# Issuing an attention stage's maxima rows and loads from SyncE in a written order

## The chip, the cores and the metric

The kernel runs on one NeuronCore of a Trainium2 chip. The metric is device time in microseconds (us), the median of several executions; less is better. One execution was also taken by the hardware profiler. The engines are TensorE (PE, with its weight loads shown apart as PEld), VectorE (DVE), ScalarE (ACT), GpSimd (POOL) and SyncE (SP), which does no arithmetic here and only issues DMAs.

## The reference, cut to what matters

Three stages follow one another, all in float32: an attention over 8 batches, 8 heads, 576 positions and 64 columns with a mask by blocks of 64; a mixture of 8 experts with a capacity of 576 tokens each; and a dense layer pair with a cosine gate.

```python
scores = np.matmul(q, k.transpose(0, 1, 3, 2)) / np.sqrt(D)
scores = np.where(mask, scores, -1e9)
scores = scores - np.max(scores, axis=-1, keepdims=True)
attn = np.exp(scores); attn = attn / (attn.sum(-1, keepdims=True) + 1e-9)
x = np.matmul(attn, v)                      # then (B*S, H*D)
x = moe(x, w_gate, w1, w2)                  # 8 experts, 576 tokens each
h = x @ w_in; out = (h * np.cos(h)) @ w_out
```

The change is in the attention alone.

## The kernel before, in words

**Pairs and groups.** The attention goes through 32 pairs of heads, `p` = 0 to 31, four pairs to a batch. A group `g` = 2p + h is one head's turn, so a pair takes an even group (h = 0) and an odd one (h = 1). In a group PE makes the scores of head g (L239, L240, tile `sT`), the product of the weights of head g - 1 with v (L288, tile `av`), and the scores of head g + 4 once more, roughly, for the row maxima only (`mx_unit`, L169, tile `mx`).

**The maxima.** `mx_unit` writes five results in each group into a rotation of three PSUM banks (`mx`, bufs=3), and DVE reduces each of them to a column of maxima (L176). So the fourth result of a group needs the bank of the first, and the fifth that of the second. In the even group, `crow(p + 1)` transposes the maxima of the next pair on PE (L203), DVE negates them into a small tile `ct` (L205), and a DMA writes them as row 64 of that pair's `QK` tile (L206), where the score product reads them as one more row to sum over. That DMA is issued by POOL.

**Split q and k.** Each pair's q and k come twice: `load_max` (L87, issued by POOL) rounds them into `QK`, and `load_raw` (L103, issued by SP) brings the unrounded values into a tile `R` (two buffers). `rests` subtracts the two, half on POOL (L144) and half on DVE (L142), into the tile `QX`.

**The order of work.** The two strings `ORDER` list the steps of an even and an odd group. PE, DVE, ACT and POOL run under `manual_schedule`: each executes its own instructions in the order in which the code traces them. In an even group POOL therefore has: `load_max(p + 3)`, the row's DMA (step `c`), and `rests(p + 1, 1)` (step `rp`, L144). In an odd group it has one addition (L615). SP isn't under that rule: a scheduler placed its DMAs, which may stand before or after their place in the code; a load can be issued as soon as its buffer is free.

**Held loads.** `hold` (L350) is a copy by DVE of one element of the newest `ct` into the tile that a load is about to fill. The load then has to wait for that copy, and with it for the maxima. From group 10 on, `vT` (L153) and the weight tiles `w` (L599) are held so, at step `L`.

**Side work.** The 64-bit words of the dense layer's weights are turned into float32 on the way: for each chunk a load (L599), a `split` at the end of an odd group on DVE (L607, L608, L609), an addition on POOL two groups later (L615) and, at step `D` of the even group after that, a last DVE instruction (L627) and a store (L628). At the first pair of each batch `store_x` also adds two reductions on DVE for the router (L328, L329) and stores the finished batch.

```python
ORDER = ("x1 D s0 a0 a1 s1 c rc m0 x2 L a2 s2 m1 m2 a3 rp s3 m3 m4 k s4 a4 v rd A0",
         "x1 s0 a0 a1 s1 c rc m0 x2 a2 s2 m1 m2 B a3 s3 m3 m4 k s4 a4 v A1")
```

`x1` and `x2` are the sums and the normalization (L297, L298, L308, L310), `s` the score products with their exponentials, `a` the products with v, `m` the maxima products, `rd` the DVE half of `rests`, `A` the split, `D` the store.

Of the kernel before, what the change touches and what calls it, by code (L numbers as in the profile page):

```python
# [12 lines left out]
def _warn_once_fixed(msg, *args, **kwargs):  # L13
# [6 lines left out]
F32 = mybir.dt.float32  # L20
F32R = mybir.dt.float32r
# [3 lines left out]
OP = mybir.AluOpType  # L25
# [3 lines left out]
B, H, S, D = 8, 8, 576, 64  # L29
# [11 lines left out]

PR = dict(EC=3, E2=2, E5=7, GC=0, SI=1, NX=3, LV=3, Q0=2, WM=14, WE=0, SW=1, W0=16, WG=0, WN=5, PA=0, CS=2, sT=2, mx=3, tr=1, e32=3, RO=0, XO=0, SO=0, GO=200, TPS=4, SEP=5, L2=3, L5=9, LAG=3, WK=3, XG=5, BIG=16, GLD=99, IW=4, W1=14, CW=1, XS=6, AH=3)
PA = [(), (2, 5), (1, 3, 5), (0, 2, 4)][PR['PA']]
ORDER = ("x1 D s0 a0 a1 s1 c rc m0 x2 L a2 s2 m1 m2 a3 rp s3 m3 m4 k s4 a4 v rd A0",
         "x1 s0 a0 a1 s1 c rc m0 x2 a2 s2 m1 m2 B a3 s3 m3 m4 k s4 a4 v A1")


# [6 lines left out]
def attention(ctx, tc, qk, vv, vt, cmask, wg, xs, lg, ident, wu, side, late):  # L54
# [5 lines left out]
    nc = tc.nc  # L60
# [139 lines left out]
    def crow(p):  # L200
        n = "mx" if p < 3 else "tr"
        pt = P.tile([128, 512], F32, name=n, bufs=PR[n])
        nc.tensor.transpose(pt[0:10, 0:128], NM[p][:, 0:10], ident)  # L203
        ct = CT[p] = W.tile([10, 128], F32, name="ct")
        nc.vector.tensor_scalar(ct, pt[0:10, 0:128], -1.0, None, op0=OP.mult)  # L205
        nc.gpsimd.dma_start(QK[p % NQ][64:65, 0].rearrange("o h (c n) -> o (h c) n", c=5), ct)  # L206

    NZ = EX[2][:, 0:325].rearrange("p (c n) -> p c n", c=5)

# [138 lines left out]
    def hold(t):  # L348

        nc.vector.tensor_copy(t, CT[max(CT)][0:t.shape[0], 0:1])  # L350
# [103 lines left out]
    for g in range(NHD + 2):  # L454
        p, h = divmod(g, 2)
        b, pr = divmod(p, 4)
        on = g < NHD
        if on and b + 1 < B and g % 8 in (5, 7):
            u = 0 if g % 8 == 5 else 4
            if b == 0:  # L460
                hold(VB[1][0:1, 0, u, 0:1])
                hold(VB[1][0:1, 4, u, 0:1])
            load_v(b + 1, u, u + 4)
        if g == 0:
            start()
            continue
        if on and h == 0 and p + 1 < NP:
            if p == 2:
                hold(VT[1][0:1, 0:1])
            if p < 6:  # L470
                load_vt(p + 1)
        if on and h == 0:
            if p > 1 and p + 3 < NP:
                load_max(p + 3)
            if p == 1:
                zero(0, nc.gpsimd)
                mask(0)
            if p > 3 and p + 2 < NP:
                load_raw(p + 2)
        work = side(g)  # L480
        if on and h == 0 and 4 < p < NP - 2:
            def early(p=p):
                hold(VT[p % 2][0:1, 0:1])
                load_vt(p + 2)
            work["L"] = [early] + work.get("L", [])
        gms = [x for x in MX.get(g, [g + 4]) if x < NHD]

        def m(u):
            for x in gms:
                mx_unit(x, u)  # L490

        def s(t):
            if on:
                sc_unit(g, t)

        def a(j):
            if 0 <= g - 1 < NHD:
                av_part(g - 1, j)

        def c():  # L500
            if h == 0 and 1 < p + 1 < NP and p != 1:
                crow(p + 1)

        def x1():
            if 0 <= g - 2 < NHD:
                sums(g - 2)

        def x2():
            if 0 <= g - 2 < NHD:
                norm(g - 2)  # L510
            if g % 8 in (2, 3) and g > 3:
                store_x(b - 1, g % 8 - 2)

        more = on and 0 < p and p + 1 < NP

        def rc():
            if more:
                copies(p + 1, h)

        def rd():  # L520
            if more:
                rests(p + 1, 0)

        def rp():
            if more:
                rests(p + 1, 1)

        def v():
            q = p + 1 if h == 1 and p + 1 < NP else None
            if q is not None:  # L530
                for j in range(5):
                    vg_unit(q, j)

        def k():
            for x in gms:
                if x % 2:
                    crow_max(x // 2)

        def V():
            for j in range(5):  # L540
                vg_unit(1, j)

        did = {"P0": lambda: rest_pair(1, 0), "P1": lambda: rest_pair(1, 1), "L3": lambda: load_max(3), "L4": lambda: load_max(4),
               "R0": lambda: row_part(1, 0, 4, 1), "R1": lambda: row_part(1, 4, 5, 1), "Y0": lambda: copies(1, 0), "Y1": lambda: copies(1, 1),
               "T0": lambda: round_pair(2, 0), "T1": lambda: round_pair(2, 1), "X0": lambda: head_max(0, NM[1]), "X1": lambda: head_max(1, NM[1]), "Z": lambda: zeros(2, nc.gpsimd), "Z1": fourth, "H6": lambda: load_raw(5), "C1": lambda: crow(1), "C": lambda: crow(2),
               "H": held, "H4": later_pair, "V": V, "x1": x1, "x2": x2, "c": c, "rc": rc, "rd": rd, "rp": rp, "v": v, "k": k}
        order = ORDER[h]
        if 0 < g < 4:
            order = (FIRST, SECOND, THIRD)[g - 1]
        if g == 6:  # L550
            order = order.replace(" c ", " c H6 ")
        if g > 59:
            order = LATE if g == 60 else LATE.replace("rd rp ", "")
            if g >= NHD:
                order = "x1 a0 a1 x2 D a2 a3 a4"
        for w in order.split():
            if w in did:
                did[w]()
            elif w[0] in "ABDL":
                for f in work.pop(w[0], ()):  # L560
                    f()
            elif w[0] == "M":
                mx_unit(int(w[1]), int(w[2]))
            elif w[0] == "G":
                vg_unit(0, int(w[1]))
            elif w[0] in "sam" and len(w) == 2:
                {"s": s, "a": a, "m": m}[w[0]](int(w[1]))
        for w in work.values():
            for f in w:
                f()  # L570
        if g > 5:
            late()
# [6 lines left out]
def to_single(ctx, tc, srcs, dst):  # L579

    nc = tc.nc
    V, G = nc.vector, nc.gpsimd
    W = ctx.enter_context(tc.tile_pool(name="cv_w", bufs=2))
    C = ctx.enter_context(tc.tile_pool(name="cv_c", bufs=1))
    top = C.tile([128, 1], I32, name="top")
    V.memset(top, -(1 << 30))
    st = {}  # L590

    first = sorted(list(range(7, 64, 2)) + [6, 60, 62])

    def load(c, h=False):
        st[c] = [W.tile([128, 512, 2], I32, name="w64", bufs=3)]
        a = st[c][0]
        if h or c < 3:
            side.hold(a[0:1, 0, 0:1])
        nc.sync.dma_start(a, srcs[c].rearrange("p (n t) -> p n t", t=2))  # L599

    def split(c):
        a = st[c][0]
        hi, lo = a[:, :, 1], a[:, :, 0]
        t = W.tile([128, 512], I32, name="w32", bufs=3)
        r = W.tile([128, 512], I32, name="wrd", bufs=2)
        st[c] += [t, r]
        V.tensor_scalar(t, hi, 0x07FFFFFF, 3, op0=OP.bitwise_and, op1=OP.logical_shift_left)  # L607
        V.scalar_tensor_tensor(t, hi, top[:, 0:1], t, op0=OP.bitwise_and, op1=OP.bitwise_or)  # L608
        V.tensor_scalar(r, lo, 28, None, op0=OP.logical_shift_right)  # L609

    def rounds(c):
        a, t, r = st[c]
        nc.scalar.activation(r, r, AF.Copy, scale=0.5)
        if c < 31:
            G.tensor_tensor(t, t, r, op=OP.add)  # L615

    def size(c):
        a = st[c][0][:, :, 1].bitcast(F32)
        g = W.tile([128, 512], F32, name="wab", bufs=1) if c < 30 else a
        nc.scalar.activation(g, a, AF.Abs)  # L620
        st[c].append(g)

    def store(c):
        a, t, r, g = st.pop(c)
        if c == 31:
            V.tensor_tensor(t, t, r, op=OP.add)
        V.scalar_tensor_tensor(t.bitcast(F32), g, MIN64, t.bitcast(F32), op0=OP.is_ge, op1=OP.mult)  # L627
        nc.sync.dma_start(dst[c], t.bitcast(F32))  # L628

    def middle(c):  # L630
        rounds(c)
        size(c)

    def side(g):
        work = {}
        for c, f in enumerate(first):
            late = 2 if f > 61 else 1 if f > 58 or f < 7 else 0
            if g == f - (2 if f > 58 or f < 10 else 3):
                if 9 < g < 58 and g % 2 == 0:
                    work.setdefault("L", []).append(lambda c=c: load(c, True))  # L640
                else:
                    load(c)
            for n, d, w in (("A", f, split), ("B", f + 2 - late, middle), ("D", f + 3 - late, store)):
                if g == d:
                    work.setdefault(n, []).append(lambda w=w, c=c: w(c))
        return work
    return side
# [682 lines left out]
```

## Time and profile before

| what | value |
|---|---|
| median of 3 runs | 1683.81 us (1680.65 to 1686.99) |
| the profiled execution | 1681.19 us |
| its span, first to last instruction | 1679.3 us |
| mean granted TensorE clock | 0.990 |
| attention's even and odd groups of the middle | about 12.2 us for the two together |

The profiled execution lies 2.6 us under the median of the runs. "Busy" is the time in which an engine had an instruction of its own in work; instructions of one engine overlap by some hundredths of a microsecond at their ends. In the timelines, a bracket shows how long the engine was idle before a group of instructions and which instruction ended that.

### The profile page before, as it was taken

What the parts mean: (1) busy time and instruction counts of PE and PEld (TensorE: products, weight loads), DVE (VectorE), ACT (ScalarE), POOL (GpSimd) and SP (SyncE); (2) the same over time, 40 slices, a digit from 0 to 9 for tenths busy, and PEclk for the clock granted to TensorE, in tenths of its full rate; (3) what the DMA queues carried; (4) which work ended last, traced back from release to release, by engine and by line L of the source; (5) the groups of instructions that cost most, each with busy time, mean ns of one, the idle gap of its engine ahead of it and who ended that gap; (6) DMA issues with size and microseconds to landing.
All of it is one profiled execution on the core that took longest, in us unless ns stands there. A gap on an engine that the chain in (4) does not pass through costs nothing.

```text
span 1679.3 us, 29421 instructions
## 1 busy us (share of the span) xinstructions
PE 1655.3 (99%) x10852; PEld 1478.8 (88%) x10852; DVE 1087.9 (65%) x2946; ACT 808.7 (48%) x1622; POOL 293.9 (18%) x259
## 2 busy tenths in 40 slices
PE   9999999998899999999999999999999999999998
PEld 7999999997698898899889889988988988998886
DVE  6888888887769777676667667677554343433342
ACT  6566666664345634443442544344254344434443
POOL 7344443432124400100100100100110000000000
PEclk9999999998799999999999999999999999999999
DMA  8999899975442333423423433433433333323332
GB/s 164 293 236 233 238 253 245 232 197 184 138 157 107 119 95 107 123 96 93 132 87 100 126 88 101 132 89 104 120 120 93 99 103 98 98 84 98 113 107 82
DMA packets 112510, 230.25 MB, mean 137 GB/s; under 512 B 12989, under 2 KB 23667, under 8 KB 110339
## 3 DMA queue, kind: packets, MB, share of 16 engines
q1 hardware_dynamic: 97344, 191.21, 39.2%
q0 software_dynamic: 15024, 37.17, 9.3%
q8 instruction: 86, 1.41, 0.4%
q14 instruction: 56, 0.46, 0.1%
HBM read 192.52 MB, written 35.65 MB: 136 GB/s over the span
## 4 chain that ended last, share of the span: by engine, by line
PE 91%; issue 6%; DVE 2%; POOL 1%; ACT 0%; POOLq 0%; DVEq 0%
PE wk L1093 21%; PE acc L1118 21%; PE acc L1066 12%; PE av L288 10%; PE wk L1041 7%; PE acc L1041 4%; PE sT L239 3%; PE mx L169 3%; PE sT L240 3%; PE tr L271 2%; PE rt L1026 1%; PE rt L926 1%; PE wk L1203 1%; PE rt L800 1%; PE av L354 0%
## 5 line engine op out<-in xcount | busy, mean ns | idle before, releaser
L1118 PE MATMUL acc<-wh,big 128*128 128x512 f32 x1136 | 375.4, 392 | 0.0
L1118 PEld LDWEIGHTS acc<-wh,big 128*128 128x128 f32 x1136 | 212.6, 188 | 42.9
L1093 PE MATMUL wk<-yh,wh 128*128 128x512 f32 x576 | 227.9, 396 | 0.0
L288 PE MATMUL av<-vb,e 128*128 128x100 f32 (+1 forms) x1920 | 224.5, 259 | 0.0
L1093 PE MATMUL wk<-yh,win 128*128 128x512 f32 x576 | 224.4, 390 | 0.0
L1093 PE MATMUL wk<-yl,wh 128*128 128x512 f32 x576 | 224.4, 390 | 0.0
L1118 PE MATMUL acc<-wout,big 128*128 128x512 f32 x568 | 222.6, 392 | 0.0
L1096 ACT ACTIVATE big<-wk 128x512 int32<-128x512 f32 x144 | 85.8, 596 | 281.3 <-PE wk L1093 270.2
L1099 DVE SCALAR_TENSOR_TENSOR big<-big,wk 128x512 f32<-128x512 int32 x144 | 98.7, 685 | 186.8 <-ACT big L1096 186.7
L288 PEld LDWEIGHTS av<-vb,e 128*128 128x128 f32 (+1 forms) x1920 | 208.5, 173 | 4.1 <-ACT vb L275 0.2
L258 ACT ACTIVATE e<-sT 128x288 f32<-128x288 f32 (+3 forms) x320 | 132.3, 424 | 97.4 <-PE sT L240 90.9
L1066 PE MATMUL acc<-big,wh 128*128 128x288 f32 x1024 | 179.0, 297 | 0.0
L176 DVE TENSOR_REDUCE nm<-mx 128x1 f32<-128x288 f32 (+1 forms) x374 | 144.1, 429 | 48.7 <-PE mx L169 45.9
L993 DVE TENSOR_TENSOR wl<-wr,wh 128x512 fp32r<-128x512 f32 x128 | 88.2, 691 | 108.2 <-PE acc L1066 38.1
L1127 POOL DMA_INDIRECT out<-big,idx x36 | 35.7, 993 | 681.4 <-ACT big L1124 673.6
L1066 PEld LDWEIGHTS acc<-big,wh 128*128 128x128 f32 x1024 | 149.9, 189 | 0.1
L1104 DVE TENSOR_TENSOR big<-wk,big 128x512 f32<-128x512 f32 x144 | 99.3, 690 | 78.0 <-ACT big L1101 77.7
L992 ACT ACTIVATE wh<-wr 128x512 fp32r<-128x512 f32 x128 | 81.0, 633 | 106.0 <-DMA wr<-in_w 38.5
L239 PE MATMUL sT<-qk 128*128 128x288 f32 (+5 forms) x384 | 128.2, 343 | 0.4 <-ACT qk L220 0.2
L1093 PEld LDWEIGHTS wk<-yh,win 128*128 128x128 f32 x576 | 108.1, 188 | 22.9
L1093 PEld LDWEIGHTS wk<-yh,wh 128*128 128x128 f32 x576 | 108.5, 188 | 21.2
L1093 PEld LDWEIGHTS wk<-yl,wh 128*128 128x128 f32 x576 | 108.3, 188 | 20.9
(255 smaller groups left out, 3105.8 us busy)
## 6 DMA issues: line engine op xcount, KB each, us to landing
wh<-hs SPq DMA_DIRECT2D x256, 256.0 KB, 2.6
wr<-in_w SPq DMA_DIRECT2D x128, 256.0 KB, 2.7
R<-in_qk SPq DMA_DIRECT2D x30, 576.0 KB, 6.8
qk<-in_qk POOLq DMA_DIRECT2D x29, 576.0 KB, 6.2
vT<-in_vt SPq DMA_DIRECT2D x32, 288.0 KB, 3.9
w<-in_win SPq DMA_DIRECT2D x16, 512.0 KB, 5.2
ws<-w SPq DMA_DIRECT2D x32, 256.0 KB, 4.1
xs<-X SPq DMA_DIRECT2D x16, 512.0 KB, 7.3
```

Of the source, the lines that this page charges most:

```text
L176: RED.append(nc.vector.tensor_reduce(m[:, c:c + 1], ps[:, o:o + n], axis=AX.X, op=OP.max))
L239: nc.tensor.matmul(out, lhsT=a[0:r, 1, h, k], rhs=a[0:r, 0, h, 64 + q0:64 + q0 + n], start=True, stop=False)
L258: nc.scalar.activation(e[:, o:o + n], ps[:, 0:n], AF.Exp, scale=0.125)
L288: nc.tensor.matmul(AV[hg % 2][0:n, c, w], lhsT=E32[hg][:, q:q + n], rhs=v[:, (j * H + hd) * 73 - o + w.start:(j * H + hd) * 73 - o + w.sto ...
L993: V.tensor_sub(l,raw,h.bitcast(F32))
L1041: nc.tensor.matmul(ps[q][:,0:288],lhsT=w[:,128*d:128*d+128],rhs=x[:,d,288*q:288*q+288],start=d==0 and n==0,stop=d==3 and n==2)
L1066: nc.tensor.matmul(ps[q][:,0:288],lhsT=w[:,sl],rhs=x[:,288*q:288*q+288],start=f==0 and n==0,stop=f==7 and n==2)
L1093: nc.tensor.matmul(ps,lhsT=w[:,sl],rhs=y[:,d,:],start=d==0 and n==0,stop=d==3 and n==2)
L1096: A.activation(k,ps,AF.Copy,scale=1/(2*math.pi))
L1099: V.scalar_tensor_tensor(r,k,-2*math.pi,ps,op0=OP.mult,op1=OP.add)
L1104: V.tensor_tensor(r,ps,r,op=OP.mult)
L1118: nc.tensor.matmul(acc[t],lhsT=g[:,128*t:128*t+128],rhs=w,start=c==0 and n==0,stop=c==15 and n==2)
```

## The change

The DMA of the maxima row goes to SP for pairs 6 to 28 instead of POOL. For it, `ct` is written as float32r and the DMA sees both sides as float32. For groups 10 to 55 SP, too, is put under `manual_schedule`. The loads of step `L` (`vT` and `w`) now stand right behind the row, and their held copies go away. The unrounded q and k (`load_raw(p + 2)`) move from the start of the even group to the start of the odd group, which in SP's order is behind the row, `vT`, `w` and, where a batch's v is loaded, behind that too.

```diff
-ORDER = ("x1 D s0 a0 a1 s1 c rc m0 x2 L a2 s2 m1 m2 a3 rp s3 m3 m4 k s4 a4 v rd A0",
+ORDER = ("x1 D s0 a0 a1 s1 c rc m0 x2 a2 s2 m1 m2 a3 rp s3 m3 m4 k s4 a4 v rd A0",
...
-        ct = CT[p] = W.tile([10, 128], F32, name="ct")
-        nc.vector.tensor_scalar(ct, pt[0:10, 0:128], -1.0, None, op0=OP.mult)
-        nc.gpsimd.dma_start(QK[p % NQ][64:65, 0].rearrange("o h (c n) -> o (h c) n", c=5), ct)
+        c = W.tile([10, 128], F32R, name="ct")
+        CT[p] = c.bitcast(F32)
+        nc.vector.tensor_scalar(c, pt[0:10, 0:128], -1.0, None, op0=OP.mult)
+        e = nc.sync if 5 < p < 29 else nc.gpsimd
+        e.dma_start(QK[p % NQ][64:65, 0].bitcast(F32).rearrange("o h (c n) -> o (h c) n", c=5), CT[p])
...
+        if g == 10:
+            loads = ExitStack()
+            loads.enter_context(tc.manual_schedule(engines={T.SP}))
+        if g == 56:
+            loads.close()
+        if h and 4 < p < 28:
+            load_raw(p + 2)
...
-            if p > 3 and p + 2 < NP:
+            if p == 4 or 27 < p < NP - 2:
                 load_raw(p + 2)
...
             def early(p=p):
-                hold(VT[p % 2][0:1, 0:1])
                 load_vt(p + 2)
...
                 crow(p + 1)
+            for f in work.pop("L", ()):
+                f()
...
-                    work.setdefault("L", []).append(lambda c=c: load(c, True))
+                    work.setdefault("L", []).append(lambda c=c: load(c))
```

## Rows read from the trace of the kernel before

**Rows 1.** The page: busy time, share of the span, instructions.

```profile
PE 1655.3 (99%) x10852; PEld 1478.8 (88%) x10852; DVE 1087.9 (65%) x2946; ACT 808.7 (48%) x1622; POOL 293.9 (18%) x259
```

**Rows 2.** Windows, the attention's middle: length, busy time by engine (instructions), clock, DMA.

```profile
110.00:360.00 250.00, 250.00 (x2199) 243.54 (x2198) 211.84 (x607) 158.89 (x371) 104.53 (x84) 1.00 0.92 236
```

**Rows 3.** POOL's timeline, one pair: start, length, line, tiles [idle before <-what ended it].

```profile
245.42 0.66 POOL L87 DMA_DIRECT2D qk<-in_qk  x1
248.53 0.53 POOL L206 DMA_DIRECT2D qk<-ct  x1 [2.45 <-DVE ct L205]
249.12 2.64 POOL L144 TENSOR_TENSOR qx<-R,qk 64x1152 fp32r<-64x1152 f32 x1
```

**Rows 4.** DVE's timeline in the same even group.

```profile
245.87 0.75 DVE L608 SCALAR_TENSOR_TENSOR w<-w,top,w 128x512 int32<-128x512 int32 x1
246.53 0.42 DVE L609 TENSOR_SCALAR wrd<-w 128x512 int32<-128x512 int32 x1
...
247.17 0.67 DVE L627 SCALAR_TENSOR_TENSOR w<-wab,w 128x512 f32<-128x512 f32 x1
247.96 0.28 DVE L205 TENSOR_SCALAR ct<-tr 10x128 f32<-10x128 f32 x1
248.17 0.48 DVE L176 TENSOR_REDUCE nm<-mx 128x1 f32<-128x64 f32 x2
...
248.67 0.48 DVE L310 TENSOR_TENSOR X<-av,r 128x320 f32<-128x320 f32 x1
249.07 0.13 DVE L350 COPY vT<-ct 1x1 f32<-1x1 f32 x1
```

**Rows 5.** Groups of DVE instructions by shape in the middle: count, busy us, mean ns, idle.

```profile
L176 DVE TENSOR_REDUCE nm<-mx 128x1 f32<-128x320 f32 x41 | 20.0, 489 | 7.2 <-PE mx L169 5.1
```

**Rows 6.** PE's timeline in that group: first scores; fourth and fifth maxima products.

```profile
246.37 0.38 PE L239 MATMUL sT<-qk 128*128 128x288 f32 x1
...
250.58 0.43 PE L169 MATMUL mx<-qk 128*128 128x288 f32 x2
```

**Rows 7.** POOL's timeline in the dense stage.

```profile
509.54 1.67 POOL L1002 TENSOR_TENSOR win<-win,wh 128x512 fp32r<-128x512 f32 x1 [0.71 <-ACT wh L1001]
```

**Rows 8.** DVE's timeline in the same stretch.

```profile
509.37 0.69 DVE L1106 TENSOR_TENSOR big<-big 128x512 fp32r<-128x512 f32 x1
509.98 1.31 DVE L749 TENSOR_TENSOR rj<-ri,fmask 128x56 int32<-128x56 int32 x1
```

**Rows 9.** DVE's timeline at the attention's end.

```profile
393.52 0.69 DVE L627 SCALAR_TENSOR_TENSOR w<-wab,w 128x512 f32<-128x512 f32 x1 [2.14 <-POOL w L615]
...
397.59 1.75 DVE L627 SCALAR_TENSOR_TENSOR w<-wab,w 128x512 f32<-128x512 f32 x1 [1.12 <-POOL w L615]
```

**Rows 10.** POOL's timeline there, two additions in one row.

```profile
396.28 2.51 POOL L615 TENSOR_TENSOR w<-w,wrd 128x512 int32<-128x512 int32 x2 [2.79 <-ACT wrd L613]
```

**Rows 11.** DVE's timeline, two instructions of the same kind and shape.

```profile
536.11 1.21 DVE L903 TENSOR_SCALAR pm<-pp 128x36 int32<-128x36 int32 x1
537.24 0.17 DVE L906 TENSOR_SCALAR pi<-pp 128x36 int32<-128x36 int32 x1
```

**Rows 12.** POOL's timeline beside them.

```profile
535.99 1.30 POOL L1002 TENSOR_TENSOR wout<-wout,wh 128x512 fp32r<-128x512 f32 x1
```

**Rows 13.** DVE's timeline in the first pair of a batch: the router's reductions.

```profile
224.66 0.63 DVE L328 TENSOR_REDUCE lg<-lgh 128x32 f32<-128x256 f32 x1
225.30 0.27 DVE L329 TENSOR_REDUCE lg<-lgh 64x8 f32<-64x64 f32 x1
```

**Rows 14.** SP's DMA issues around one pair.

```profile
239.80 0.38 SPq L147 DMA_DIRECT2D vb<-in_vv  x1
240.88 0.47 SPq L103 DMA_DIRECT2D R<-in_qk  x1
```

**Rows 15.** The 20 loads of `R` (L103) in the middle, issue to landing.

```profile
DMA to landing us min/median/max: 5.0/6.6/8.1
```

**Rows 16.** The 21 maxima rows (L206) in the middle, issue to landing.

```profile
DMA to landing us min/median/max: 2.5/3.7/5.9
```

## The prediction

> **What bounds the kernel now.** I read the page first: PE is busy for 99% of the span [rows 1]. A busy PE can still hide waits, so next the windows over the attention's middle, the stretch that the change touches. There PE has work in 250.00 of 250 us, its weight loads in 243.5 of them, at full clock; DVE has 211.8, POOL 104.5 [rows 2]. The list of PE's waits is empty in that stretch. So the middle has nothing to give: whatever the change takes from DVE, POOL or SP there is taken from idle time. It can only cost, and it costs where PE is made to wait. DVE is the engine to watch, since its spare time is 38.2 us in the 250. With 41 groups in the stretch [rows 5] a group lasts 6.1 us and a pair 12.2, so DVE has 1.9 us to spare in a pair. Last come the timelines of POOL, DVE and PE over one even group [rows 3, 4, 6], to see what the row's DMA holds up on POOL, and what stands beside it.
>
> **The held copies** cost DVE 0.13 us each [rows 4], two in a pair, 0.26 us. PE waits for none of it: gain 0.
>
> **The row on SP.** Only the issuer changes. The row is issued behind `ct` at 248.24 (247.96 + 0.28) [rows 4] and is read by the next pair's first scores, at 246.37 + 12.2 = 258.6 [rows 6]: 10.3 us. It took 2.5 to 5.9 on POOL's queue [rows 16]; the larger loads of SP's queue landed in at most 8.1 [rows 15]. Both are hidden: 0. What stands behind it on SP are `vT`, `w`, v and R, each wanted about a pair later: 0.
>
> **R later in SP's order.** R is now issued up to a pair later, behind v where v is loaded. Before, one R stood behind v at 240.88 [rows 14]; at 5.0 to 8.1 us [rows 15] such a load lands at 245.9 to 249.0, by the median at 247.5. Its reader on DVE (L142) starts only behind all of the group's maxima, past 251; POOL's reader L144 is free until the next even group. No one on PE's path waits: 0.
>
> **What POOL does without the row.** Here I see the price. In the even group POOL issues `load_max` (until 246.08), then stands 2.45 us for `ct`, issues the row at 248.53, and only then subtracts, L144, 249.12 to 251.76 [rows 3]. L144 itself reads R and `QK`, not the row: the row's place ahead of it is all that keeps it there. With the row gone, L144 is ready 0.06 us (the gap behind the row's DMA) after `load_max`, at 246.14: three microseconds earlier. Where it stands now, DVE reduces PSUM banks. Where it will stand, DVE has L608, L609 and L627, which work from SBUF to SBUF [rows 4].
>
> Do the two engines get in each other's way? The trace has such meetings. L627, 0.69 us alone, takes 1.75 when POOL's addition runs beside it, and ends at 399.34, 0.55 us behind the addition's end at 398.79 [rows 9, 10]. L903, with one SBUF input, takes 1.21 beside a subtraction of POOL (535.99 to 537.29) and ends at 537.32; its twin L906 takes 0.17 [rows 11, 12]. The other way round, POOL's subtraction at 509.54 met L1106, which had begun first and ended at 510.06; it took 1.67 instead of 1.30 and ended 1.15 behind L1106, while L749, issued next on DVE, had to wait for POOL and ended at 511.29 [rows 7, 8, 12]. So the later one waits, in full, and a waiting POOL comes before DVE's next instruction.
>
> The Trainium skill has this rule: SBUF — State Buffer, section "Who interferes with whom", says that DVE and GpSimd share a port pair under an exclusive lock, that a DVE instruction with two SBUF inputs or in a two-port mode takes part, and that a reduction doesn't. It speaks against this change. By its words on two-input instructions alone, with L609 let through, the cost would be that of the second rival; by the rows on L903 it is the sum below.
>
> **The sum for one pair.** L608 holds until 246.62 [rows 4]. L144 then needs 2.64 less the 0.15 that the waiting one had already behind it (1.30 - 1.15): it ends at 249.11. L609 ends 0.28 later (0.42 less the 0.14 that L627 saved, 0.69 - 0.55): 249.39. From L609's end to L627's start 0.22 as now, L627 0.67: 250.28. From there to the end of the first maxima reductions 0.81 now (247.84 to 248.65); 0.12 of it is the wait for PE, gone by then, so I take 0.65 to 0.7: 250.95. Normalization to L310's end 0.50: 251.45. The copies are gone; the second reduction, 0.49 [rows 5] with an overlap of 0.1: 251.84. Its bank is wanted by the fifth product, which now starts at 250.71 (250.58 + 0.43 - 0.30) [rows 6]. So PE stands 1.1 us in this group. What is late next is the row, by 2.3 us of its slack, and the stores; neither matters. In the first pair of a batch the router's reductions, 0.90 us, stand ahead of the second reduction too [rows 13]: 2.0 us.
>
> Bounds for a pair: if L609 isn't held, L627 ends at 249.11 + 0.55 = 249.66, 0.62 earlier: 0.5. Above, a weight load of some 0.2 us between the freed bank and the product: 1.3. If R lands after L627's start (247.17), L144 waits for that load instead and meets reductions: 0.
>
> How many pairs? Rows go to SP for 23 of them, groups 10 to 54. In 12 no v is loaded ahead of R. R is then issued a good microsecond earlier than at 240.88 and, at 6.6 us, has landed before 246.14: 6 first pairs of a batch at 2.0 and 6 others at 1.1, 18.6 us. In the 11 with v, R lands at 245.9 to 249, about half of that ahead of L627: 11 x 0.55 = 6.1. Together 24.7 us. On the profiled execution's 1681.19 (span 1679.3 and 1.9 around it) that makes 1705.9; the median of the runs lies 2.6 above that execution, so the median after should be 1708.
>
> **The rivals.**
>
> *No collision (not slower).* R, now last in its pair, lands behind 247.2 in most pairs, or L144 is kept back by something that I don't see; then L144 stays beside the reductions. For it: in half of the pairs R is behind v, the DMA engines are 92% busy [rows 2], and the collision is decided by 1 us. Against it: the median landing. Time: 1684, within the scatter of the runs or a few us above. Chance 0.24.
>
> *Only two-input instructions wait.* Then 0.5 instead of 1.1 and 1.4 instead of 2.0, a quarter in the pairs with v: 6 x 1.4 + 6 x 0.5 + 11 x 0.25 = 14 us, 1698. Against it stands L903. Chance 0.17, slower too.
>
> *The row comes late behind SP's bulk.* PE would stand at the next pair's first scores. It decides from 10.3 us (8.0 if `ct` is late by 2.3), where 8.1 was the worst load. At 1 us late in each pair: 23 us on top, 1730. Chance 0.03.
>
> The Trainium skill, DMA: Bandwidth & Descriptors, section "Queues, rings and completion order", says that one issuer's transfers are taken in ring order; by that the row goes behind the store issued just ahead of it, which bears on this rival alone. No row here shows a small transfer on SP's queue.
>
> *Faster.* PE has no wait to lose in the middle, and outside of it the change touches nothing on PE's path. 0.04 for the runs' own scatter.
>
> **Chances and range.** The collision as summed has 0.52, with the lighter form 0.69, the late row 0.03: slower 0.72. No collision makes 0.24 same, and faster is left with 0.04. By over or under 0.5%, 8.4 us, a measurement of this kernel can tell a change from none. The collision's own range is 1695 (0.5 and 1.4 in the 12 pairs without v, 11 us) to 1719 (1.3 and 2.2 in all 23, 35 us). To leave out no more than 2 in 10, the range must reach into the case without: 1681 to 1719.
>
> **What would show it.** After: L144 starts right behind `load_max`, some 3 us earlier against PE; L609 or L627 grows from 0.4 or 0.7 to over 2 us; PE gets gaps ahead of L169 released by DVE's L176, about 1 us a pair, twice that at a batch's start; a pair lasts 13.3 us. The prediction is wrong if L144 waits for R instead, if DVE's instructions keep their lengths beside it, or if PE's gaps stand at the scores.

## Result and the profile after

The changed kernel takes 1701.76 us (median of 6 runs, 1698.07 to 1703.8) beside 1684.19 us (6 runs, 1680.65 to 1686.99) for the kernel before on the same chip: ratio 1.0102, 95% interval 1.0086 to 1.0117. It is slower, by 17.6 us at the median; 1708 was predicted. The profiled execution took 1700.66 us with a span of 1698.9, 19.6 above the span before.

In the listing of the changed kernel some lines have moved. L144, L142, L169 and L176 are the same; the third split instruction, L609 before, is now L619; the product with the sizes, L627 before, is L637; POOL's addition is L625; the reciprocal of an even group, from which I measure below, is L300. In the experiments the third split instruction is L622 (the gate), L611 (the row alone), L617 (raw q and k early) and L614 (two halves, where the subtraction is L145 and the product L632).

The first view of after is the window over the attention's middle (length, then busy time of PE, PEld, DVE, ACT, POOL with counts, clock, DMA share, GB/s), answering to [rows 2]:

```profile
110.00:360.00 250.00, 240.77 (x2065) 230.88 (x2065) 218.18 (x534) 149.51 (x347) 90.19 (x58) 0.99 0.88 225
```

PE, which had work in all 250 us, now lacks 9.2 us of it, and it got through 2065 matmuls instead of 2199. DVE is busier although 73 instructions fewer ran in the stretch.

The list of waits in the same stretch (who, line, what it waits for: us, times, longest) says who stood. PE had no line there before:

```profile
POOL qx L144 <- DMA R<-in_qk: 23.1, 10, 4.8
PEld mx L169 <- DVE nm L176: 13.1, 17, 1.6
PE mx L169 <- DVE nm L176: 9.1, 13, 1.4
```

The groups by shape in that stretch say what grew on DVE. L619 was 421 ns on average and is 1193; L637 was 668 and is 898; the reductions of [rows 5] keep their length, 487 beside 489:

```profile
L144 POOL TENSOR_TENSOR qx<-R,qk 64x1152 fp32r<-64x1152 f32 x20 | 55.6, 2781 | 36.0 <-DMA R<-in_qk 23.1 <-ACT e L260 7.9 <-DMA qk<-ct 3.8
L142 DVE TENSOR_TENSOR qx<-R,qk 64x1152 fp32r<-64x1152 f32 x20 | 31.9, 1593 | 0.0
L619 DVE TENSOR_SCALAR wrd<-w 128x512 int32<-128x512 int32 x19 | 22.7, 1193 | 0.0
L176 DVE TENSOR_REDUCE nm<-mx 128x1 f32<-128x320 f32 x38 | 18.5, 487 | 6.6 <-PE mx L169 6.2
L637 DVE SCALAR_TENSOR_TENSOR w<-wab,w 128x512 f32<-128x512 f32 x19 | 17.1, 898 | 0.2 <-ACT e L260 0.2
```

An average over pairs hides that there are two kinds of pair. Here is one of the first kind, group 26, on the timelines of POOL, DVE and PE (start, length, engine, line, tiles), to be laid beside [rows 3, 4, 6]:

```profile
182.29 0.63 POOL L87 DMA_DIRECT2D qk<-in_qk  x1
183.06 2.93 POOL L144 TENSOR_TENSOR qx<-R,qk 64x1152 fp32r<-64x1152 f32 x1
```

```profile
182.74 0.75 DVE L618 SCALAR_TENSOR_TENSOR w<-w,top,w 128x512 int32<-128x512 int32 x1
183.41 2.88 DVE L619 TENSOR_SCALAR wrd<-w 128x512 int32<-128x512 int32 x1
...
186.39 0.19 DVE L300 RECIPROCAL r<-r 128x5 f32<-128x5 f32 x1
186.49 0.67 DVE L637 SCALAR_TENSOR_TENSOR w<-wab,w 128x512 f32<-128x512 f32 x1
...
188.18 0.59 DVE L330 TENSOR_REDUCE lg<-lgh 128x32 f32<-128x256 f32 x1
188.69 0.24 DVE L331 TENSOR_REDUCE lg<-lgh 64x8 f32<-64x64 f32 x1
188.87 1.73 DVE L176 TENSOR_REDUCE nm<-mx 128x1 f32<-128x320 f32 x4
```

```profile
187.80 0.40 PE L169 MATMUL mx<-qk 128*128 128x288 f32 x1 [0.20 <-DVE nm L176]
189.39 0.40 PE L169 MATMUL mx<-qk 128*128 128x288 f32 x1 [1.20 <-DVE nm L176]
```

POOL's subtraction is ready right behind `load_max`, gets going while L618 holds, and L619, 0.42 us alone, lasts until 186.29, 0.30 behind the subtraction's end at 185.99. Everything behind L619 on DVE is late by 2.46 us; the router's reductions come on top, and PE stands for 1.40 us (0.20 and 1.20) at the last two maxima products. The subtraction overlaps L618 by 0.43 us and is 0.29 longer than alone, so it waited too, for DVE.

The other kind of pair is group 32. POOL's subtraction and the load it waits for, on the timelines of SP and POOL:

```profile
214.57 0.52 SPq L148 DMA_DIRECT2D vb<-in_vv  x1
215.19 0.54 SPq L103 DMA_DIRECT2D R<-in_qk  x1
...
225.50 0.49 SPq L103 DMA_DIRECT2D R<-in_qk  x1
```

```profile
225.36 2.64 POOL L144 TENSOR_TENSOR qx<-R,qk 64x1152 fp32r<-64x1152 f32 x1 [4.00 <-DMA R<-in_qk]
233.98 2.65 POOL L144 TENSOR_TENSOR qx<-R,qk 64x1152 fp32r<-64x1152 f32 x1 [0.43 <-DMA R<-in_qk]
```

The load issued behind v at 215.19 lets the subtraction go at 225.36, 10.2 us later; by then the reductions are running and nothing is held. The one issued at 225.50, in a pair without v, has landed at 233.98, 8.5 us after its issue, in time for the collision in group 34. Over the 23 pairs, on DVE's timeline: in 8 the third split instruction is held to 2.87 us (the first pairs of all six batches, and the two behind the first two of them), in 2 it is the product with the sizes, 2.85 us (groups 36 and 52), and 13 escape, all 11 with v among them. In each of the 13 the trace has R's load finished 0.16 to 0.17 us before the subtraction starts, also where its line above names an exponential (L260) or the maxima row's DMA: those ended within 0.16 us of the load.

### The profile page after: what moved, and what is told of

Its sections match the earlier page's. It is cut to its first block, busy times and chain, and to the rows that moved or that the text cites. A ratio compares the mean times of both kernels' runs of the same rounds, so it can differ in the third digit from the quotient of the medians.

```text
span 1698.9 us, 29332 instructions
## 1 busy us (share of the span) xinstructions
PE 1662.0 (98%) x10852; PEld 1481.5 (87%) x10852; DVE 1112.5 (65%) x2898; ACT 809.0 (48%) x1622; POOL 285.5 (17%) x236
## 3 DMA queue, kind: packets, MB, share of 16 engines
q8 instruction: 86, 1.41, 0.4%
## 4 chain that ended last, share of the span: by engine, by line
PE 85%; issue 7%; DVE 4%; DMA 2%; ACT 1%; SPq 0%; POOL 0%; POOLq 0%; ACTq 0%
PE wk L1103 21%; PE acc L1128 21%; PE acc L1076 12%; PE av L290 9%; PE wk L1051 7%; PE acc L1051 4%; PE sT L241 3%; PE mx L169 2%; PE sT L242 2%; PE tr L273 1%; DVE wrd L619 1%; DVE nm L176 1%; PE rt L1036 1%; DMA X<-in_qk 1%; DMA xs<-X 1%
## 5 line engine op out<-in xcount | busy, mean ns | idle before, releaser
L260 ACT ACTIVATE e<-sT 128x288 f32<-128x288 f32 (+3 forms) x320 | 132.4, 424 | 117.0 <-PE sT L242 111.2
L176 DVE TENSOR_REDUCE nm<-mx 128x1 f32<-128x288 f32 (+1 forms) x374 | 142.7, 426 | 45.3 <-PE mx L169 44.3
```

The costliest lines, as they stand in the source:

```text
L176: RED.append(nc.vector.tensor_reduce(m[:, c:c + 1], ps[:, o:o + n], axis=AX.X, op=OP.max))
L260: nc.scalar.activation(e[:, o:o + n], ps[:, 0:n], AF.Exp, scale=0.125)
```

## Experiments

The pair's period is read from the starts of the even groups' reciprocals on DVE's timeline. Over the 24 pairs from group 8 to group 56 the kernel before needed 292.1 us, 12.17 a pair. The changed one needs 312.4, 20.3 more, which is the whole of the 19.6 that its span is longer:

```profile
64.20 0.19 DVE L300 RECIPROCAL r<-r 128x5 f32<-128x5 f32 x1
...
376.63 0.19 DVE L300 RECIPROCAL r<-r 128x5 f32<-128x5 f32 x1
```

My theory: the earlier start of POOL's subtraction costs all of it, where it meets DVE's instructions from SBUF to SBUF. The rivals: the late raw q and k cost it, or the row on SP, or the order on SP.

### The gate: after, with the subtraction kept behind `ct`

```diff
         e = nc.sync if 5 < p < 29 else nc.gpsimd
         e.dma_start(QK[p % NQ][64:65, 0].bitcast(F32).rearrange("o h (c n) -> o (h c) n", c=5), CT[p])
+        if 5 < p < 29:
+            gt = W.tile([1, 1], F32, name="gt")
+            nc.gpsimd.tensor_copy(gt, CT[p][0:1, 0:1])
```

> The changed kernel, but POOL copies one element of ct right behind load_max in each even group whose row SP issues, so that its subtraction (L144) again cannot begin before ct is written. Collision theory: L144 starts about 2 us behind the sums, the third split instruction keeps 0.42 us, PE has no waits for L176, the time is that of the kernel before, 1680 to 1687. Rival, SP's written order or the late R: POOL's copy changes neither, so 1698 to 1704 stays.

Measured: 1680.49 us (1679.32 to 1681.14), ratio to the kernel before 0.9976, interval 0.9961 to 0.9992. It is faster than the changed kernel by 21 us and, beside the 1683.88 of the kernel before (19 runs), than that by 3: less than the bound of 0.5%, though the interval leaves out 1. In the attention the 3 us are not gained: from group 8 to group 56 this kernel needs 292.0 us, the kernel before 292.1. POOL and DVE in one of its even groups:

```profile
183.63 0.63 POOL L87 DMA_DIRECT2D qk<-in_qk  x1
186.51 0.17 POOL L210 COPY gt<-ct 1x1 f32<-1x1 f32 x1 [2.25 <-DVE ct L206]
186.76 2.65 POOL L144 TENSOR_TENSOR qx<-R,qk 64x1152 fp32r<-64x1152 f32 x1
```

```profile
184.75 0.42 DVE L622 TENSOR_SCALAR wrd<-w 128x512 int32<-128x512 int32 x1
```

A copy of one element, which does nothing but wait, gives back all that was lost: POOL stands 2.25 us, and DVE's L622 is back at 0.42. The row on SP, SP's order, the late raw q and k and the missing held copies are all in this kernel, so none of them is what costs.

### The row alone: before, with nothing but the row on SP

```diff
-        nc.gpsimd.dma_start(QK[p % NQ][64:65, 0].rearrange("o h (c n) -> o (h c) n", c=5), ct)
+        e = nc.sync if 5 < p < 29 else nc.gpsimd
+        e.dma_start(QK[p % NQ][64:65, 0].bitcast(F32).rearrange("o h (c n) -> o (h c) n", c=5), CT[p])
```

> The kernel before with one part of the change: the maxima rows of pairs 6 to 28 go out on SP; held copies, the scheduler's order of SP and the early R stay. Collision theory: R has landed long before, so L144 starts behind load_max in all 23 pairs and each costs what the colliding pairs cost in the changed kernel, about 2 us: 1684 + 35 to 50, 1719 to 1734, slower than the whole change. Rival, SP's written order or the late R is what costs: this keeps the old order, so 1680 to 1690.

Measured: 1722.45 us (1718.19 to 1726.71), ratio 1.0217, interval 1.0167 to 1.0266. One part of the change costs more than the whole. Its groups in the middle:

```profile
L144 POOL TENSOR_TENSOR qx<-R,qk 64x1152 fp32r<-64x1152 f32 x18 | 54.4, 3024 | 1.1
L611 DVE TENSOR_SCALAR wrd<-w 128x512 int32<-128x512 int32 x18 | 51.7, 2870 | 0.0
```

All 18 pairs of the stretch collide, and POOL stands 1.1 us in all ahead of its subtractions instead of 36.0: here raw q and k are still loaded early. A pair lasts 13.53 us where nothing else is in the way, 1.36 more than 12.17. From group 8 to group 56 the profiled execution (1726.3 us) lost some 46 us, 2.0 a pair, as forecast, but not evenly: a plain pair paid 1.36, and a batch's first pair 3.6 to 3.9, because all six have the bout at a lower clock that the last section tells of. The forecast knew of no such bout; that it was met is in part luck.

### The order alone: after, with the rows back on POOL

```diff
-        e = nc.sync if 5 < p < 29 else nc.gpsimd
+        e = nc.gpsimd
```

> The changed kernel with the rows back on POOL: SP keeps the written order, the late R and no held copies. Collision theory: L144 stands behind the row again, 1680 to 1687. Rival, SP's order or the late R costs: nearly the whole loss stays, 1695 to 1704.

Measured: 1681.2 us (1680.32 to 1688.13), ratio 0.9982, interval 0.9964 to 1.0. SP's written order, raw q and k last and the loads without held copies cost nothing. PE has its 250.00 us of work in the middle again:

```profile
110.00:360.00 250.00, 250.00 (x2199) 243.61 (x2199) 209.81 (x566) 159.08 (x371) 104.55 (x84) 1.00 0.92 238
```

DVE's 2.0 us and 41 instructions less than in [rows 2] are the held copies, and they bring nothing. In this run the landings of R in the middle can be read, and in the written order they come later after the issue than in [rows 15]:

```profile
DMA to landing us min/median/max: 6.7/8.8/9.9
```

### The subtraction alone: before, with `rp` ahead of `c`

```diff
+        if h == 0 and 9 < g < 56:
+            order = order.replace(" a3 rp ", " a3 ").replace(" c ", " rp c ")
```

> The kernel before with one step moved in the written order and nothing else: in the even groups 10 to 54 POOL's subtraction (rp) stands ahead of the row (c), so no DMA changes its issuer or its place. Collision theory: L144 runs right behind load_max in all 23 pairs as in e2: 1719 to 1734. Rival, the loss comes from anything that SP does: 1680 to 1690, with the row some 2.7 us later on POOL and hidden.

Measured: 1722.88 us (1720.8 to 1730.36), ratio 1.0242, interval 1.0193 to 1.029. No DMA has changed its queue or its order here; two steps of POOL have changed places. The middle looks like that of the row alone, 13.53 us a pair. On POOL's timeline the row is still there, behind the subtraction:

```profile
201.37 0.66 POOL L87 DMA_DIRECT2D qk<-in_qk  x1
202.09 2.98 POOL L144 TENSOR_TENSOR qx<-R,qk 64x1152 fp32r<-64x1152 f32 x1
206.72 0.53 POOL L206 DMA_DIRECT2D qk<-ct  x1 [1.65 <-DVE ct L205]
```

So the place of the subtraction is sufficient by itself.

### Raw q and k early: after, with their load at the even group's start

```diff
-        if h and 4 < p < 28:
-            load_raw(p + 2)
...
-            if p == 4 or 27 < p < NP - 2:
+            if p > 3 and p + 2 < NP:
                 load_raw(p + 2)
```

> The changed kernel with one thing put back: the load of raw q and k is traced at the even group's start again, ahead of v and of the big loads, so that it lands earlier; the row of maxima stays on SyncE and nothing is held. By the theory that the pairs without a collision escaped only because raw q and k landed late: GpSimd's subtraction is ready behind load_max in nearly all 23 pairs, the third split instruction (or the product with the sizes) is held to some 2.85 us there, the period is 13.5 us instead of 12.17 in steady pairs, and the time goes up from 1702 to 1715-1728 us, slower than the changed kernel although its loads come earlier. By the rival that the late load itself costs the changed kernel its 18 us: the time falls to that of the kernel before, 1681-1687 us. By the rival that the place of the load is irrelevant: 1699-1704 us.

Measured: 1716.23 us (1714.49 to 1718.14), ratio 1.0194, interval 1.0175 to 1.0213. Landing earlier costs nearly 1% more than the changed kernel's 1.0102, as the theory wants and neither rival does:

```profile
L144 POOL TENSOR_TENSOR qx<-R,qk 64x1152 fp32r<-64x1152 f32 x18 | 54.3, 3018 | 1.1
L617 DVE TENSOR_SCALAR wrd<-w 128x512 int32<-128x512 int32 x18 | 51.7, 2872 | 0.0
```

Every pair collides again. A plain pair lasts 13.40 us here and not 13.53: the two held copies of the kernel before, which took 0.13 us out of DVE's chain between the normalization and the second reduction, are gone, and DVE sets the time in a pair that collides: PE's gap at the fifth maxima product is 0.50 us here and 0.62 in the row alone. They are worth nothing only where nothing collides.

### Two halves: the subtraction alone, cut into its two heads

```diff
+        elif 5 < p < 29:
+            for h in range(2):
+                nc.gpsimd.tensor_sub(x[64:128, 1, h, 64:640], r[:, 1, h], a[:, 1, h].bitcast(F32))
```

> The kernel before with GpSimd's subtraction of q ahead of the row of maxima in even groups (the kernel of e4, 1722.9 us), but the subtraction is cut into its two heads, two instructions of some 1.3 us. By the theory that VectorE's instruction is held until the one GpSimd instruction in progress has ended: the third split instruction takes 1.5-1.9 us instead of 2.87, the second half holds a later one of VectorE's instructions or none; a pair pays 0.1-0.5 us instead of 1.36 where the second half finds no partner, and the time is 1684-1697 us. By the rival that the held instruction waits for all of GpSimd's work in a row, or that VectorE's instructions are slowed in proportion to GpSimd's columns whatever their cut: 2.8 us again and 1715-1728 us. By the rival that each half holds another instruction for its whole length, the sum is the same as without the cut: 1710-1723 us.

Measured: 1717.19 us (1714.53 to 1721.33), ratio 1.0209, interval 1.0185 to 1.0233. My own forecast for this run, 1684 to 1697, was wrong. The time lies in the second forecast and in the third; L614 at 1.64 us, and not 2.8, speaks for the third. The groups by shape:

```profile
L145 POOL TENSOR_TENSOR qx<-R,qk 64x576 fp32r<-64x576 f32 x36 | 59.8, 1678 | 1.1
L614 DVE TENSOR_SCALAR wrd<-w 128x512 int32<-128x512 int32 x18 | 29.5, 1637 | 0.0
L632 DVE SCALAR_TENSOR_TENSOR w<-wab,w 128x512 f32<-128x512 f32 x18 | 29.1, 1616 | 0.0
```

The first half holds L614 for 1.22 us beyond its 0.42, the second holds L632 for 0.95 beyond its 0.67. The two engines take turns: an instruction waits for the one in progress and not for all of the other's queue, but the cut lets the second half find the next partner. The sum, 2.17 us instead of 2.45, is nearly the same, and so is the pair, 13.25 us.

## Why the prediction was right, and where not

**The mechanism held.** Step by step, for the 10 pairs that collide: the subtraction starts right behind `load_max` in 7 of them, and 0.4 to 0.7 us later, when R has landed, in groups 34, 36 and 52; L609 as was (now L619) is held in 8, as L903 had been in [rows 11], so not two-input instructions alone; PE's new gaps stand at L169 released by L176, not at the scores. The Trainium skill's SBUF — State Buffer, section "Who interferes with whom", has the lock between the two engines; the runs agree with it in that L176's mean beside it stays at 487 ns. The gate and the subtraction alone show cause in both directions: take the early start away and the loss is gone, bring it alone and the loss is there.

**The price of a pair held.** For a plain pair 1.1 us was summed, with bounds of 0.5 and 1.3. The runs give 1.23 (raw q and k early) and 1.36 (row alone, with the held copies). For a batch's first pair it was 2.0: the changed kernel paid 1.9 to 2.2 in the four that stand by themselves, groups 26, 34, 42 and 50, each taken over two periods (14.63 + 11.65 less 2 x 12.17 for group 26). Where it was L637 that was held, about 0.97. The gaps in PE's timeline show less than a wait costs: group 26 has 1.40 us of them and paid 1.9. A maxima product that waits stands alone, 0.40 us, while two in a row took 0.43 [rows 6], and its weight load waits with it (the line `PEld mx L169` in the list of waits).

**The count of pairs failed as a term of the sum.** The step said that raw q and k land 5.0 to 8.1 us after their issue [rows 15], so that all 12 pairs without v collide and half of the 11 with v. In the changed order they stand close behind the row, `vT`, `w` and v, and the subtraction is let go up to 9.0 us after the issue without v (group 28: issued at 189.96, let go at 198.54; group 44: 292.39 and 301.37) and 7.2 to 10.9 us after it with v. That the order makes the loads slower is borne out by the order alone, with a median of 8.8 us against 6.6. In three pairs with v, groups 22, 38 and 40, the load took no longer than summed, 7.2 us, but the subtraction was ready only some 0.3 us behind L637's start. All 11 with v escaped, 0 instead of 6.1 us, and so did groups 28 and 44 of the others. The 12 without v paid 20.3 us in place of 18.6, of which some 3 come from the clock, told below. The sum had no term for the clock: two errors of opposite sign, 6.1 us too much and some 3 too little, bring 24.7 as near to 20.3 as it is, and that much is luck. The rival without a collision was thus right for 13 of 23 pairs, by its first reason: the load lands late. The late load, a by-product of the change, hid about half of what the row's move costs; with the load early it would have been 1716.

**The edits costed at nothing** are at nothing: SP's order, the late load and the row's new issuer by the gate and the order alone, the held copies by the order alone. The row did not come late: no wait of PE at the scores stands in the list. One thing that I had not named is hidden as well: where the subtraction comes late it meets DVE's own, L142, whose mean rises from 1340 to 1593 ns. In groups 30, 46 and 54 it takes 2.08 to 2.92 us and the pair lasts 12.17 all the same; only in group 14, with 3.05, does PE wait 0.13 us at L169, and the pair lasts 12.31 instead of 11.88.

What stays open: the records show lengths and ends, and not who holds what. That it is a port, and not something else which the two engines share, is inferred and wasn't tried.

## What to carry to other kernels

An instruction that waits for nothing it needs may still be a gate: before a DMA is taken off an engine's queue, ask what is behind it there, when that would start by itself, and what another engine does at that time. A load that comes late can be what keeps two engines apart, so a change of two parts should be run part by part; here one part hid about half of the other's loss. When two engines take turns, cutting one's instruction moves the loss to the next instruction, while moving it beside work that doesn't take part removes it, here at the price of a copy of 0.17 us on an engine with time to spare.

## What the runs showed of the hardware

The granted clock can fall for a short bout in the middle of the attention. Of the changed kernel's six first pairs of a batch two have it, groups 10 and 18. PE's longer gap in group 18, and windows around it (same columns as above):

```profile
136.12 0.40 PE L169 MATMUL mx<-qk 128*128 128x288 f32 x1 [1.42 <-DVE nm L176]
...
134.00:136.00 2.00, 0.51 (x2) 0.19 (x1) 1.96 (x7) 0.44 (x1) 0.00 (x0) 1.00 0.35 134
136.00:138.00 2.00, 1.88 (x17) 1.76 (x18) 2.00 (x5) 0.43 (x2) 0.00 (x0) 0.89 0.92 252
138.00:140.00 2.00, 2.00 (x12) 2.00 (x11) 0.84 (x3) 0.41 (x1) 0.00 (x0) 0.50 0.99 300
```

PE had stood for 0.19 and 1.42 us at L169; behind that the clock is 0.50, 1.2 GHz instead of 2.4, although PE is busy all the time again. Group 34, with gaps of 0.19 and 1.41, stays at 1.00 throughout, as do groups 26, 42 and 50:

```profile
240.25 0.40 PE L169 MATMUL mx<-qk 128*128 128x288 f32 x1 [1.41 <-DVE nm L176]
...
238.00:240.00 2.00, 0.64 (x3) 0.19 (x1) 1.96 (x7) 0.44 (x1) 0.00 (x0) 1.00 0.36 135
240.00:242.00 2.00, 1.75 (x17) 1.64 (x18) 2.00 (x5) 0.43 (x2) 0.00 (x0) 1.00 0.65 179
242.00:244.00 2.00, 2.00 (x19) 2.00 (x18) 1.62 (x7) 1.18 (x3) 0.00 (x0) 1.00 0.91 301
```

So the same gaps came with a bout and without one, and what decides it isn't shown. With raw q and k early, a batch's first pair with such a bout (group 34) lasts 15.83 us where two without last 14.33 (groups 18 and 50), all three with gaps of 0.18 and 1.42: 1.5 us. So the price of a gap isn't its length alone; by this estimate the two bouts make some 3 of the 20.3 us.
